# A scan-and-gate kernel with a written-out issue order: whole-row loads, an exclusive scan, two accumulator tiles and a new issue table

## The chip, the cores and the metric

The kernel runs on 1 core of one Trainium2 chip. The metric is the device time of one execution in microseconds (us). The core has TensorE (PE in the rows; its weight loads are PEld), VectorE (DVE), ScalarE (ACT), GpSimd (POOL) and SyncE (SP), which here issues all of the kernel's DMAs. All data are float32; matrices for large products are held as two float32r parts, high and low, and every large product is three matmuls (high x high, high x low, low x high).

## The reference

Two parts follow each other. The first is a linear recurrence for each batch `b` and head `h` (4 batches, 8 heads, 768 steps, 48 channels):

```python
for t in range(S):
    cur = np.einsum('bhd,bhe->bhde', u[None] * kt, vt)       # the bonus u
    y[:, :, t] = np.einsum('bhd,bhde->bhe', rt, state + cur)
    state = wt[:, :, :, None] * state + np.einsum('bhd,bhe->bhde', kt, vt)
```

The second takes y as `x` (4 x 768 x 384), computes `relu(x @ w_in)` with 1024 columns, halves it into u and v, normalizes v over its 512 columns, multiplies it by `w_spatial` (768 x 768) along the steps, adds `b_spatial`, gates u with it and multiplies by `w_out` (512 x 384).

## The kernel before, in words

The steps are cut into 24 slots (4 batches x 6 chunks of 128 steps). In a slot, `slot_load` (L372) brings W (the decays), kr (k and r) and v, from slot 6 on also N (k and r the other way round). `slot_prep` (L401) makes the recurrence a matmul: it multiplies neighbouring decays into W2 (L432), scales k and r (L435), runs two product scans of DVE, F from the end of each half chunk (L438) and E from its start (L444), and scales k by F (L450) and r by E (L454). As E holds products up to and including its step, r is multiplied by E one place further on, and the first place of each half chunk is multiplied by `z0` in an operation of its own (L447). `slot_a` (L507) multiplies k with r, `slot_kt` (L528) transposes k into KT, `slot_y` (L544) and `slot_inter` (L581) accumulate y, `slot_d`, `slot_s` and `slot_w` (L597 to L640) carry the state, `slot_x` (L644) adds y's two parts and transposes y into xT.

y is accumulated in one PSUM tile `pyw` (L277) of two banks: `slot_x` copies bank 0 to SBUF (L658) and then adds bank 1 (L660). Columns 384 and up of bank 0 are `pw`, into which `warm` (L878) multiplies zeros where TensorE has nothing to do.

The second part is units of work: `hv_unit` (L689: v and its statistics), `scale` (normalization), `g_unit` (L756: u, the product with `w_spatial`, the gate) and `out_unit` (L795: the last product, the copy L807 and the store L809). `split64` (L330) splits a weight matrix that arrives as float64 into its two parts: a load (L335), a first conversion (L350) and further operations; `prep_sp` (L320) does it for `w_spatial`.

**The order of the work is written out by hand.** Each operation names the engines on which it may run and a cost for each. The string `PLAN` (L31) has one word per operation, in the order in which the code names them: a letter for the engine (T, V, A, G, S for TensorE, VectorE, ScalarE, GpSimd, SyncE) and a due time in base 36, in hundredths of a us. `plan` (L198) sorts the operations by due time, and `issue` puts them out in that order, so each engine runs its own operations strictly in the table's order. An operation that waits holds up everything behind it on its engine. A due time is not waited for. `fill` (L882) puts a number of `warm` matmuls into gaps of TensorE's due times, up to a certain operation. A load can't be issued before the users of the buffer that it fills are done; v and W have two buffers each, kr has three.

Of the kernel before, what the change touches and what calls it, by code (L numbers as in the profile page):

```python
# [16 lines left out]
C = 128  # L17
# [14 lines left out]
Txx S4g Tfy Aij Vk8 S2i9 S1r9 S5k Alg Vo5 Vpe Vuo Awp G11w Sod A1ez V1k7 V1nq V1r4 A1t5 G1vn Sm5 A14o V1ba  # L32
V1dd V1l4 A1nc V1z7 S28 S3c S8w Vfx Tkv Vb4 Gis Vhl Vcd Gej Vfb Vij Vp2 Vmh Vku Ay5 A13b V2s V10g Tpt V13h Tol
Aq2 T128 T15q Tw8 Vzp A10t V16e T1ba A1cp V1ft T1k0 A1rw T1tg A1uu Sso A1qa V1uh V22j V2da A2if V2lm Szx A23g
V2cd V2px V2sk A2v8 V2ye Sq9 A1kh V1mt V1pf V1st A20n V2na S1se A3wa G3xy S3le A4lu V4y2 S22o A4ha V4j2 S4cf
A53w V55g S4fx A5d3 V5er S4nh A5by V5ks S576 A5ka V5oq S2ww A5nx V5rp S1p1 A2te V303 S5gj A5p2 V5t0 S4zt A5fd
G5x6 S5mi A5xe G6d7 S2ll A37y V3km V3n2 V3pc A44p V4re S2h5 V31e V3ab V3fk V3iy A3v5 V4lp S3r2 V4gn V4kd V4sq
V4ud A50e V5d5 S2uo A3d2 V4vo V4wr V5bu A5e8 V5hr T1we T1zf T21t A26f A2dx A2ek S7s S6o Sa0 Vr3 Tt8 Vtq Gwl
Vsr Vwc Gyi Vzd V11s V175 Gz1 G16m Ayu A16a G3m Vy1 T19t V1h4 A17h T143 A19z T1hl T1lk T1c4 V1f2 A1gk V1vf
T1na A1p9 V1w5 T1yb A1zl T21c A22e T26w T2gs T2j9 A2rh A2wn A2xb Sl1 Sn9 S1dw V19l T1oo V15g V1c7 G1fa V17f  # L40
V1d5 V1ix V1xh V1jm G1h8 V20v A251 A25q V276 T23q V28i A1wi T1ko A1m5 T2bt T2do T25i V2ab A2bf V2gy T2fe A2hd
V2it T2l6 A2mf T2oo A2pq T2rn T2tj T2vg A2zf A31p A32c A34t V35z V35r G3dw G3eo V3fd G3hm G3ie A3m4 A3tq G429
A3q0 A3zb G48k A3j3 A4cb G56z Syt S1cs S1nx G25e T29e V248 G29d V2be V25h G28u V2b2 V2f9 V2ez G2f7 G2vf A2uj
A2go V2k5 T30j V365 A2ju T2lx A2nh T2mt T3ao T2yt V331 A35c V389 T3ce A3fe V3gv T3jm A3l2 T3n7 A3o9 T3qz T3sw
T3vo A45u A484 A48s S1xv S1q5 S2g1 G2i2 T2p6 V2rm V2u9 V2oz V2wi V325 V32o V342 V33s G32l G36e A3t1 A2qs V2v7
T3f5 V3uc A39c T39s A3bu T3p4 T3xl T3ds V3i7 V3qn V3z5 T3zb A41a V42r T46v V48c T4ao A4dq T4fa T4h7 T4jl A4mz
A4p9 A4pw S2jd S2kh S3d1 V3b1 T3gm V39d V3re V3cq V3do G3h3 V3kb V3ld V3zw V3so G3uk A3pb A3ym V3w5 T40p V44t
V419 T3ut A3xf T450 T47k T426 V442 V47k T49a A4b9 V4cp T4el A4g8 T4j4 A4ks T4me T4oa T4q7 A4sp A4v0 A4vn A4y4
V505 V4ze V4zx V50n V516 V51p V528 A57i A5aj V5g3 V5ak A5gi V5j3 V52s A551 V5m3 T8xw S3ka A42c S456 A4if S4l9
A51j S54d A5hx T2xd T320 T340 A3gg T58v T5lw T5nc T5q8 T5ro T5t4 V5wx V62k A648 V6hy T35g T36w T38c A3ec T5br  # L50
T5d7 T5en T5kg T5os T5w0 V63w V68k A6dj V6k7 T3kb T3lr T3no A3rz T5yw T60c T61s T638 T664 T6dd V6fe G6lr A6oo
# [12 lines left out]
S5p5 S6vu S7q5 S837 G6og G779 V7bw V6vz V740 V75w V78w V7je V7cu G7jn V847 V85v V87i A9az V8z3 A8fm V89j V8fl
V93e A8g3 T8rw V94o V8zo T8d3 V8fq T9ev T8tc V90r G91z V96u T9gl A9sx V9w6 T9za Va0j Va26 Taet Tahz Tajw Aame
Aaoo Aapc S6km S862 S898 S8rz V7ay V8hc G8qo V7eu G7hg V7jp V7mq V94c G8is V8vf G8ln V8ol V8q8 V9zu A9is V8rv
A8rw A98i A8zj V9es T9hz V9tn G982 T9e0 A9hl Ta1r T9jg V9om G9rd V9sw Ta35 Aa6g Va7w Tahb Aaik Vak2 Tamh Taoe
Taqb Aast Aax3 Aay2 S7eb S8u7 S8t3 S9h9 G7vh G9fy V9as V8lv G8q5 V96h V9js V9c2 V9i5 V9mz V99h G9by V9fq G9so
A9s8 V9vo A9n4 A9he Ga0n G9ov T9zy Va5x Ga7y T9mu V9pd Tabq Ta4j Vab2 Vac4 Tadf Vafe Vah2 Talt Van6 Vaot Tas8
Tavl Taxi Ab06 Ab2h Ab3y Ab6f Vb7k Vb7d Vb7w Vb8f Vb8z Vb9h Vba1 Abdl Abfy Gbhw Vbbu Abif Gbpu Vbak Abc6 Gbe4  # L70
S9id A9v1 S9xv Aadc Sag6 Aauq Saxk Ab86 T9ku T9nq T9qm A9tz Tble Tbpq Tbsm Tbu2 Tc1b Tc5n Vc7w Vcj9 Acky Gcry
T9s2 T9ti T9uy Aa20 Tbfm Tbh2 Tbii Tbwz Tbyf Tc2r Vc4s Vcgg Acn4 Gcpa T9we T9xu Ta5d Aafp Tbjy Tbmu Tboa Tbr6
Tbvj Tbzv Vc1w Gc4v Ac7s Vcur Ta7d Ta8t Taa9 Aacb Tc73 Tc8j Tc9z Tccb Tcdr Tcf7 Vcr7 Vcxk Aczd Gd11 Td5o Td7o
Td94 Tdc1 Adfn Sdh5 Tdgd Tdht Tdll Tdn1 Vdp3 Se1q Tdal Tddh Tdex Tdj9 Adyt Se3x Tau5 Tazf Tb1r Ab6y Tc47 Tco1
Tcph Tcqx Tcse Tctu Vcz6 Vd62 Adnd Gdvs Tb6e Tbba Tbcq Abhd Te6i Teau Teca Tef7 Tegn Teir Vep9 Ger3 Aeu0 Vf8b
# [144 lines left out]
def kernel(  # L220
# [812 lines left out]
```

## Time and profile before

| what | value |
|---|---|
| median of 3 runs | 388.3 us (387.86 to 388.34) |
| the profiled execution | 388.89 us, of which the span from the first to the last instruction is 387.1 us |
| TensorE's mean granted clock | 0.977 of full speed |
| TensorE (PE), busy | 361.8 us, 93% |
| DMA, bytes | 47.76 MB, mean 123 GB/s |

A busy time is the time in which at least one instruction of the engine was under way. A row of the timeline reads: start in us from the span's start, duration, engine, line, operation, output and inputs, count of merged instructions, and in brackets the engine's idle time ahead of it with what ended it. "x82" counts every matmul instruction; a float32 matmul is two of them.

### The profile page before, as it was taken

Reading aid. Unit: us, or ns where it says so; the run is one execution under the profiler, and the core shown is the slowest. Engines: PE = TensorE matmul, PEld = TensorE weight load, DVE = VectorE, ACT = ScalarE, POOL = GpSimd, SP = SyncE. Lnnn points to the kernel's source line nnn. Section 1 sums busy time; section 2 is a strip of 40 time slices with the busy share of each in tenths; the row PEclk is TensorE's granted clock in tenths of the full one; section 3 lists DMA queues with packets and bytes.
Section 4 is the critical chain, followed back from the end, with each engine's and each line's share of the span. In section 5 each row is a group of like instructions: output and inputs, shape, how many; then the busy total and the mean of one; then the engine's idle time right before and its main releaser. Section 6 shows DMA issues by size and latency. Waiting matters only on the chain.

```text
span 387.1 us, 11326 instructions
## 1 busy us (share of the span) xinstructions
PE 361.8 (93%) x4648; PEld 331.3 (86%) x4648; DVE 294.2 (76%) x649; ACT 202.9 (52%) x563; POOL 126.8 (33%) x162
## 2 busy tenths in 40 slices
PE   7969959999988999999999899998999999999995
PEld 6857748889878989889888878888999998899995
DVE  7976867799998789767979899889887767414333
ACT  2555946987441746783353476772354355641311
POOL 3524321411234244546362233125242233041110
PEclk9997986999999999999999999999999999999999
DMA  7995474565144355641353536633245401100201
GB/s 203 266 248 155 119 222 128 155 186 158 37 140 125 110 172 159 204 126 61 87 157 87 176 99 164 195 109 88 51 135 169 142 22 45 41 22 0 68 35 66
DMA packets 29514, 47.76 MB, mean 123 GB/s; under 512 B 2450, under 2 KB 21010, under 8 KB 29458
## 3 DMA queue, kind: packets, MB, share of 16 engines
q1 hardware_dynamic: 29458, 47.00, 42.9%
q8 instruction: 37, 0.61, 0.7%
q14 instruction: 19, 0.16, 0.1%
HBM read 42.27 MB, written 4.72 MB: 121 GB/s over the span
## 4 chain that ended last, share of the span: by engine, by line
PE 49%; DVE 19%; DMA 15%; ACT 8%; issue 5%; POOL 1%; SPq 0%; ACTq 0%; DVEq 0%; POOLq 0%
PE pv L681 6%; DMA kr<-in_tr_dram 6%; PE pv L682 6%; PE pv L683 6%; DMA Nw<-in_gt_dram 5%; PE pyw L555 4%; DMA d_('wo', 0)_680<-in_w_out_dram 3%; PE ph L681 2%; PE ph L683 2%; PE ph L682 2%; PE pu L681 2%; PE pu L682 2%; PE pu L683 2%; PE po L681 2%; PE yt L664 2%
## 5 line engine op out<-in xcount | busy, mean ns | idle before, releaser
L681 PE MATMUL pv<-ws,vh 128*128 128x384 f32 x192 | 66.7, 347 | 6.5 <-ACT ot L807 2.2
L683 PE MATMUL pv<-ws,vl 128*128 128x384 f32 x192 | 64.8, 338 | 0.0
L682 PE MATMUL pv<-ws,vh 128*128 128x384 f32 x192 | 64.8, 338 | 0.0
L681 PEld LDWEIGHTS pv<-ws,vh 128*128 128x128 f32 x192 | 36.0, 188 | 9.4 <-ACT ot L807 2.5
L682 PEld LDWEIGHTS pv<-ws,vh 128*128 128x128 f32 x192 | 36.1, 188 | 0.0
L683 PEld LDWEIGHTS pv<-ws,vl 128*128 128x128 f32 x192 | 36.1, 188 | 0.0
L791 ACT CAST gh<-t 128x384 fp32r<-128x384 f32 x32 | 16.0, 512 | 36.7 <-DVE t L789 24.4
L787 DVE TENSOR_TENSOR t<-pv,b_sb 128x384 f32<-128x384 f32 x32 | 17.6, 551 | 22.9 <-PE pv L683 21.8
L681 PE MATMUL pu<-xT,wi 128*128 128x384 f32 x96 | 34.7, 362 | 0.0
L681 PE MATMUL po<-wo,gh 128*128 128x384 f32 x96 | 33.4, 348 | 0.1
L435 POOL TENSOR_TENSOR kr<-kr,W 112x256 f32<-112x256 f32 x23 | 22.8, 995 | 32.2 <-issue 10.8
L682 PE MATMUL pu<-xT,wi 128*128 128x384 f32 x96 | 32.8, 342 | 0.0
L683 PE MATMUL pu<-xT,wi 128*128 128x384 f32 x96 | 32.8, 341 | 0.0
L683 PE MATMUL po<-wo,gl 128*128 128x384 f32 x96 | 32.4, 337 | 0.0
L682 PE MATMUL po<-wo,gh 128*128 128x384 f32 x96 | 32.2, 336 | 0.0
L681 PE MATMUL ph<-wi,xT 128*128 128x512 f32 x72 | 30.8, 428 | 0.0
L683 PE MATMUL ph<-wi,xT 128*128 128x512 f32 x72 | 28.7, 398 | 0.0
L682 PE MATMUL ph<-wi,xT 128*128 128x512 f32 x72 | 28.6, 397 | 0.0
L636 ACT ACTIVATE S<-S,prod 112x48 f32<-112x48 f32 x84 | 21.2, 326 | 7.0 <-DVE S L626 6.7
L789 POOL TENSOR_TENSOR t<-t,us 128x384 f32<-128x384 f32 x10 | 10.6, 1065 | 39.0 <-DVE t L787 30.8
L710 ACT ACTIVATE hv<-ph 128x512 f32<-128x512 f32 x24 | 14.3, 595 | 15.4 <-PE ph L683 15.3
L611 PE MATMUL paw<-v,KT 64*64 64x48 f32 (+1 forms) x704 | 16.1, 216 | 5.1 <-ACT KT L542 5.1
(202 smaller groups left out, 968.2 us busy)
## 6 DMA issues: line engine op xcount, KB each, us to landing
kr<-in_tr_dram SPq DMA_DIRECT2D x24, 448.0 KB, 5.0
N<-in_nat_dram SPq DMA_DIRECT2D x18, 384.0 KB, 3.9
Nw<-in_gt_dram SPq DMA_DIRECT2D x16, 384.0 KB, 3.3
W<-in_tr_dram SPq DMA_DIRECT2D x24, 224.0 KB, 4.5
v<-in_nat_dram SPq DMA_DIRECT2D x24, 192.0 KB, 3.5
out_dram<-ot SPq DMA_DIRECT2D x24, 192.0 KB, 2.0
wst<-in_w_spT_dram SPq DMA_DIRECT2D x12, 192.0 KB, 5.1
d_('wv', 0)_146<-in_w_in_dram SPq DMA_DIRECT2D x1, 512.0 KB
```

The costliest lines, as they stand in the source:

```text
L435: op({"G": pool(half), "V": dve(half)}, lambda e, n=n: e.tensor_tensor(two(kr()[:, n])[:, :, n], two(kr()[:, n])[:, :, n], two(W())[:, :, ...
L555: nc.tensor.matmul(py()[L * a:L * (a + 1), row, D * n:D * (n + 1)], x, z, start=(a, row) not in started, stop=not left[0], skip_group_chec ...
L611: nc.tensor.matmul(pa()[rows, a, G * L + g * D:G * L + (g + 1) * D], KT()[ps, g, rows], v()[ps, hs], start=True, stop=True)
L636: e.mul(S1[i % 2][a][:, g, :], S0[:, g, :], Wc[:, g:g + 1])
L664: nc.tensor.matmul(yT()[:, k_, :], y()[:, k_ * P:(k_ + 1) * P], ident, start=k_ == 0, stop=k_ == KX - 1, is_transpose=True, skip_group_che ...
L681: nc.tensor.matmul(ps, ah, bh, start=first, stop=False)
L682: nc.tensor.matmul(ps, ah, bl, start=False, stop=False)
L683: nc.tensor.matmul(ps, al, bh, start=False, stop=last)
L710: op({"A": 0.79}, lambda: nc.scalar.activation(hv(), ph(), AF.Relu, accum_out=col(0)), r=[(ph, 0)], w=[(hv, 0), (s, 0, j)])
L787: op({"V": dve(HT)}, lambda: nc.vector.tensor_tensor(t1(), pv()[:, :HT], b_sb[:, tsl], ALU.add), r=[(pv, 0), ("b", 0)], w=[(t1, 0)])
L789: op({"V": dve(HT), "G": pool(HT)}, lambda e: e.tensor_tensor(t1(), t1(), us(), ALU.mult), r=[(us, 0)], w=[(t1, 0)], port=True)
L791: op({"A": act(HT)}, lambda: nc.scalar.copy(gh(), t1()), r=[(t1, 0)], w=[(gh, 0)])
```

## The change

1. `u_sb`, the bonus vector, is loaded in all its 128 rows by the second of its loads too, where that load left out row 0.
2. W is loaded in whole rows of 516 values (`W()` from `tr[b, c, :, 1:WE]`), where it was four pieces of 128 values a row; its readers step over the value between two pieces.
3. E becomes an exclusive product: W2 is held in one tile with a leading 0, the scan reads it one place earlier and takes the maximum after the multiplication. r is multiplied by E in one operation over all places (112x512 in place of 112x496), and the operation L447 is gone, once per slot, 24 in all.
4. `pyw` becomes two tiles of one bank each, `PY[0]` and `PY[1]`; `pw` is a part of `PY[0]`.
5. The three constants and the warm-up output of ScalarE become columns of one tile; the first memsets are two of 512 columns in place of one of 1024.
6. Some costs that the operations name are changed, as L710 from 0.79 to 0.61 and L713 from 0.86 to 0.70.
7. The table is new: 1,930 words in place of 1,954. By its letters, VectorE has 578 operations in place of 637, ScalarE 404 in place of 388, GpSimd 169 in place of 150, TensorE 624 and SyncE 155 as before. `fill` makes 51 `warm` matmuls of the new table's gaps and 39 of the old one's (two further ones are operations of the table).

```diff
-    pyw = psX.tile([P, 2, 512], F32, name="pyw")
-    pw = pyw[:, 0, DM:]
-    nc.vector.memset(pyw, 0.0)
+    W2p = p1.tile([R, G * C // 2 + 1], F32, name="W2p")
+    nc.gpsimd.memset(W2p[:, :1], 0.0)
...
+    PY = [psX.tile([P, 512], F32, name=f"py{n}") for n in range(2)]
+    pw = PY[0][:, DM:]
+    for t in PY:
+        nc.vector.memset(t, 0.0)
...
-        load(W, [0], lambda: nc.sync.dma_start(
-            W().rearrange("p (g t) -> p g t", t=C),
-            tr[b, c, :, 1:WE].rearrange("p (g t) -> p g t", t=C + 1)[:, :, :C]), R * G * C * 4)
+        load(W, [0], lambda: nc.sync.dma_start(W(), tr[b, c, :, 1:WE]), R * G * C * 4)
...
         op({"V": 0.69}, lambda: nc.vector.tensor_tensor_scan(
-            E().rearrange("p s t -> p (s t)"), zE, W2(), 0.0, ALU.max, ALU.mult),
-           r=[(W2, 0), ("z0", 0)], w=[(E, 0)])
-        op({"V": 0.19}, lambda: nc.vector.tensor_tensor(
-            seg(kr()[:, 1])[:, :, 0], seg(kr()[:, 1])[:, :, 0], z0.unsqueeze(2).broadcast_to([R, SUB * G, 2]),
-            ALU.mult), r=[("z0", 0)], w=[(kr, "r0")])
+            flat(E()), W2()[:, :half], zE, 0.0, ALU.mult, ALU.max), r=[(W2, 0), ("z0", 0)], w=[(E, 0)])
...
-        op({"V": 0.68, "G": 1.07}, lambda e: e.tensor_tensor(
-            seg(kr()[:, 1])[:, :, 1:], seg(kr()[:, 1])[:, :, 1:],
-            E()[:, :, :L2 - 1].unsqueeze(3).broadcast_to([R, SUB * G, L2 - 1, 2]), ALU.mult),
+        op({"V": 0.69, "G": 1.1}, lambda e: e.tensor_tensor(
+            seg(kr()[:, 1]), seg(kr()[:, 1]), E().unsqueeze(3).broadcast_to([R, SUB * G, L2, 2]), ALU.mult),
            r=[(E, 0)], w=[(kr, "r")], port=True)
...
-        py.make = lambda: pyw[:, :, :DM]
+        py.make = lambda: PY
...
         op({"A": act(DM, True), "V": dve(DM)}, lambda e: (e.copy if e is nc.scalar else e.tensor_copy)(
-            y(), py()[:, 0]), r=[(py, 0)], w=[(y, 0)])
-        op({"V": 0.56}, lambda: nc.vector.tensor_tensor(y(), y(), py()[:, 1], ALU.add), r=[(py, 0)], w=[(y, 0)])
+            y(), py()[0][:, :DM]), r=[(py, 0)], w=[(y, 0)])
+        op({"V": 0.56}, lambda: nc.vector.tensor_tensor(y(), y(), py()[1][:, :DM], ALU.add), r=[(py, 0)], w=[(y, 0)])
```

Words of the two tables that the prediction speaks of (due times in us, decoded):

| operation | before | after |
|---|---|---|
| first matmuls on the bonus vector (L921), TensorE | `Tfy` 5.74 | `Tgq` 6.02 |
| start of y of slot 1 (L565), TensorE | `T1hl` 19.29 | `T1ov` 21.91 |
| first `w_out` load into d (`d_('wo', 0)`, L335), SyncE | `S2ll` 33.69 | `S1je` 19.94 |
| its first conversion (L350), ScalarE | `A37y` 41.74 | `A2yj` 38.35 |
| v of slot 4 (L388), SyncE | `S2g1` 31.69 | `S2j9` 32.85 |
| W of slot 5 (L381), SyncE | `S2jd` 32.89 | `S2g8` 31.76 |
| KT of slot 4 (L542), ScalarE | `A3bu` 43.14 | `A3in` 45.59 |
| state product of slot 4 (L611), TensorE | `T3ds` 43.84 | `T3ml` 47.01 |
| v of slot 5 (L388), SyncE | `S3d1` 43.57 | `S3mk` 47.00 |
| its first use (before: ScalarE, L475; after: VectorE, L486) | `A3pb` 47.99 | `V3wv` 50.71 |
| last of the 96 products of `out_unit` (L801), TensorE | `Tql1` 344.53 | `Tqt9` 347.49 |

## Rows read from the trace of the kernel before

**Rows 1.** The page's first part: busy us, share of the span, instructions.

```profile
PE 361.8 (93%) x4648; PEld 331.3 (86%) x4648; DVE 294.2 (76%) x649; ACT 202.9 (52%) x563; POOL 126.8 (33%) x162
```

**Rows 2.** The page's fourth part: the chain of waits, by engine.

```profile
PE 49%; DVE 19%; DMA 15%; ACT 8%; issue 5%; POOL 1%; SPq 0%; ACTq 0%; DVEq 0%; POOLq 0%
```

**Rows 3.** Busy time by stretch: stretch, length, each engine's busy us, clock, DMA.

```profile
27.90:34.70 6.80, 6.47 (x27) 5.68 (x27) 4.37 (x9) 3.21 (x9) 2.50 (x2) 0.50 0.93 253
55.20:65.40 10.20, 6.79 (x83) 6.67 (x84) 7.49 (x17) 5.34 (x14) 2.11 (x4) 0.50 0.31 102
70.00:382.00 312.00, 302.86 (x3777) 280.23 (x3769) 240.85 (x528) 162.13 (x457) 103.96 (x125) 1.00 0.38 109
```

**Rows 4.** Timeline, TensorE's last product.

```profile
382.11 0.34 PE L681 MATMUL po<-wo,gh 128*128 128x384 f32 x1
```

**Rows 5.** Timeline, TensorE's first work.

```profile
2.88 4.63 PE L880 MATMUL pyw<-zk 128*128 128x128 f32 x20 [2.88 <-DVE pyw L279]
7.44 0.72 PE L921 MATMUL pu__174<-ones,u_sb 1*48 1x1 f32 x16
```

**Rows 6.** Timeline, TensorE from 19 to 34 us.

```profile
21.84 1.60 PE L880 MATMUL pyw<-zk 128*128 128x128 f32 x12 [1.71 <-DVE y L660]
23.28 0.81 PE L565 MATMUL pyw<-bv,ident 128*128 128x384 f32 x2
...
27.33 0.43 PE L555 MATMUL pyw<-S,kr 48*64 48x48 f32 x12 [1.57 <-issue]
...
31.53 1.65 PE L880 MATMUL pyw<-zk 128*128 128x128 f32 x6 [0.33 <-DVE y L660]
```

**Rows 7.** Timeline, ScalarE and VectorE on y of slot 0.

```profile
19.83 0.48 ACT L658 COPY y<-pyw 128x384 f32<-128x384 f32 x1 [0.69 <-PE pyw L555]
...
21.25 0.54 DVE L660 TENSOR_TENSOR y<-y,pyw 128x384 f32<-128x384 f32 x1
```

**Rows 8.** Timeline, TensorE's longest wait.

```profile
58.62 0.98 PE L611 MATMUL paw<-v,KT 64*64 64x48 f32 x30 [5.08 <-ACT KT L542]
```

**Rows 9.** Timeline, ScalarE ahead of it.

```profile
56.70 0.55 ACT L350 ACTIVATE e_('wo', 0)_811<-d_('wo', 0)_680 128x384 f32<-128x384 f32 x1 [5.23 <-DMA d_('wo', 0)_680<-in_w_out_dram]
...
58.05 0.51 ACT L542 COPY KT<-pt 128x448 f32<-128x448 f32 x1
```

**Rows 10.** Timeline, the loads that SyncE issues from 40 us on.

```profile
40.88 0.33 SPq L388 DMA_DIRECT2D v<-in_nat_dram  x1
...
42.12 3.14 SPq L381 DMA_DIRECT2D W<-in_tr_dram  x1
...
46.35 0.44 SPq L335 DMA_DIRECT2D d_('wo', 0)_680<-in_w_out_dram  x1
```

**Rows 11.** The page's sixth part: loads, count, KB, median us from issue to landing.

```profile
kr<-in_tr_dram SPq DMA_DIRECT2D x24, 448.0 KB, 5.0
N<-in_nat_dram SPq DMA_DIRECT2D x18, 384.0 KB, 3.9
...
W<-in_tr_dram SPq DMA_DIRECT2D x24, 224.0 KB, 4.5
v<-in_nat_dram SPq DMA_DIRECT2D x24, 192.0 KB, 3.5
```

**Rows 12.** Groups by line, VectorE: busy us, mean ns; idle before.

```profile
L432 DVE TENSOR_TENSOR W<-W 112x256 f32<-112x256 f32 x18 | 12.0, 665 | 2.3 <-DMA W<-in_tr_dram 2.2
...
L447 DVE TENSOR_TENSOR kr<-kr,zz 112x16 f32<-112x16 f32 x24 | 3.8, 160 | 0.2
```

**Rows 13.** Timeline, GpSimd and VectorE beside each other.

```profile
11.73 1.08 POOL L435 TENSOR_TENSOR kr<-kr,W 112x256 f32<-112x256 f32 x1 [4.11 <-DVE rk L411]
12.02 1.06 DVE L432 TENSOR_TENSOR W<-W 112x256 f32<-112x256 f32 x1
...
16.69 0.46 DVE L432 TENSOR_TENSOR W<-W 112x256 f32<-112x256 f32 x1
```

More of the change, by code (lines that the diff above doesn't have):

```diff
@@ L37 @@
[L37 to L51, printed above, removed]
@@ new lines @@
+T13o T15x Tx1 V10n A15e V1ej T18f A19v V1h2 T1s5 A1vc T1xl A23h Suq A1we V21n V2bl V2g0 A2qc G2xa Sng A1mu
+V1r1 V1sa V1uw A2gd V2i8 S1h0 A2kw V2n4 V2pq V2sq A2us V345 S2v6 A3to G496 S238 A3gn V439 S25r A34s V38c S3xz
+A4i8 V4r1 S4c7 A5nh V5qb S4ux A5gg V5ms S2sw A5tl G5yv S5jh A5uq V61n S1i4 A2o6 V2rf S5v7 A67e V6i0 S4jx A5af
+V5hp S4y9 A5l7 V6jc S1je A2yj V31r V32u V363 A3d0 V5co S2i5 A3ju V3m4 V3q7 V4h2 A53l V5j1 S2qm A3m6 V4gb V4pq
+V504 A5k2 V5o3 S4it V4wy V4zd V51f V55w A5mc V5rn T27w T29t T2e2 A2hs A2jk A2mh S5k S7s Sgo Vur Tyf Vlw Vwp
@@ L121 @@
+Tqkl Tqrt Tqt9 Aqvb Sqwv Vn8u Tnlb Vp1v
 """
@@ L273 @@
     z0 = zz[:R, 1, :, 0]
+    W2p = p1.tile([R, G * C // 2 + 1], F32, name="W2p")
+    nc.gpsimd.memset(W2p[:, :1], 0.0)
     AS = [p1.tile([P, 2, G, L], F32, name=f"AS{n}") for n in range(AB)]
     paw = psA.tile([P, 2, 512], F32, name="paw")
-    pyw = psX.tile([P, 2, 512], F32, name="pyw")
-    pw = pyw[:, 0, DM:]
-    nc.vector.memset(pyw, 0.0)
+    PY = [psX.tile([P, 512], F32, name=f"py{n}") for n in range(2)]
+    pw = PY[0][:, DM:]
+    for t in PY:
+        nc.vector.memset(t, 0.0)
     ident = cp.tile([P, P], F32, name="ident")
     make_identity(nc, ident)
-    ones = cp.tile([P, 1], F32, name="ones")
-    nc.gpsimd.memset(ones, 1.0)
-    eps = cp.tile([P, 1], F32, name="eps")
-    nc.gpsimd.memset(eps, EPS)
-    neg = cp.tile([P, 1], F32, name="neg")
-    nc.gpsimd.memset(neg, -1.0)
-    nc.scalar.activation(cp.tile([P, 1], F32, name="warm"), eps, AF.Sqrt)
+    few = cp.tile([P, 4], F32, name="few")
+    ones, eps, neg = (few[:, n:n + 1] for n in range(3))
+    for t, x in ((ones, 1.0), (eps, EPS), (neg, -1.0)):
+        nc.gpsimd.memset(t, x)
+    nc.scalar.activation(few[:, 3:], eps, AF.Sqrt)
     mneg = pm.tile([P, 512], F32, tag="hv", name="mneg", bufs=4)
@@ L425, in two, with flat, w_ @@
         def two(t):
-            return t.rearrange("p (n q) -> p n q", q=2)
+            return t.rearrange("p (g n q) -> p g n q", g=G, q=2)
         def seg(t):
             return t.rearrange("p (s n q) -> p s n q", n=L2, q=2)
+        def flat(t):
+            return t.rearrange("p s t -> p (s t)")
+        def w_():
+            return W().rearrange("p (g t) -> p g t", t=C + 1)[:, :, :C].rearrange("p g (n q) -> p g n q", q=2)
         half = G * C // 2
-        op({"G": pool(half), "V": dve(half)}, lambda e: e.tensor_tensor(
-            W2(), two(W())[:, :, 0], two(W())[:, :, 1], ALU.mult), r=[(W, 0)], w=[(W2, 0)], port=True)
-        for n, key in ((0, ["k"]), (1, ["r", "r0"])):
-            op({"G": pool(half), "V": dve(half)}, lambda e, n=n: e.tensor_tensor(
-                two(kr()[:, n])[:, :, n], two(kr()[:, n])[:, :, n], two(W())[:, :, 1 - n], ALU.mult),
-               r=[(W, 0)], w=[(kr, x) for x in key], port=True)
+        op({"G": 0.62, "V": dve(half)}, lambda e: e.tensor_tensor(
+            W2()[:, 1:].rearrange("p (g n) -> p g n", g=G), w_()[:, :, :, 0], w_()[:, :, :, 1], ALU.mult),
+           r=[(W, 0)], w=[(W2, 0)], port=True)
+        for n, key in ((0, "k"), (1, "r")):
+            op({"G": 0.9, "V": dve(half)}, lambda e, n=n: e.tensor_tensor(
+                two(kr()[:, n])[:, :, :, n], two(kr()[:, n])[:, :, :, n], w_()[:, :, :, 1 - n], ALU.mult),
+               r=[(W, 0)], w=[(kr, key)], port=True)
         op({"V": 0.69}, lambda: nc.vector.tensor_tensor_scan(
-            F().rearrange("p s t -> p (s t)")[:, ::-1], zF[:, ::-1], W2()[:, ::-1], 0.0, ALU.max, ALU.mult),
-           r=[(W2, 0)], w=[(F, 0)])
-        op({"V": 0.16, "G": 0.23}, lambda e: e.tensor_scalar(Wc, F()[:, :, 0], FLOOR, None, ALU.max),
+            flat(F())[:, ::-1], zF[:, ::-1], W2()[:, :0:-1], 0.0, ALU.max, ALU.mult), r=[(W2, 0)], w=[(F, 0)])
+        op({"V": 0.17, "G": 0.24}, lambda e: e.tensor_scalar(Wc, F()[:, :, 0], FLOOR, None, ALU.max),
            r=[(F, 0)], w=[("Wc", i)], port=True)
@@ L491, in slot_prep @@
         for n, (j_, src, dst) in enumerate(((0, slice(0, C), slice(0, C)), (1, *halves), (1, *halves[::-1]))):
-            op({"A": 0.17, "V": 0.14}, lambda e, j_=j_, src=src, dst=dst: (e.copy if e is nc.scalar else e.tensor_copy)(
+            op({"A": 0.19, "V": 0.165}, lambda e, j_=j_, src=src, dst=dst: (e.copy if e is nc.scalar else e.tensor_copy)(
                 dgs()[dst, j_], dg()[src, :H].rearrange("p (g j) -> p j g", j=2)[:, j_]), r=[(dg, 0)], w=[(dgs, n)])
@@ L503, in diag @@
                                     dgs()[:, j].unsqueeze(2).broadcast_to([P, G, L]), ALU.mult)
-            op({"G": 0.74, "A": 1.06, "V": 0.42}, diag, r=[(dgs, n) for n in ((0,), (1, 2))[j]], w=[(As, j)], port=True)
+            op({"G": 0.62, "A": 1.07, "V": 0.43}, diag, r=[(dgs, n) for n in ((0,), (1, 2))[j]], w=[(As, j)], port=True)
     def slot_a(i):
@@ L554, in mm @@
             left[0] -= 1
-            nc.tensor.matmul(py()[L * a:L * (a + 1), row, D * n:D * (n + 1)], x, z, start=(a, row) not in started,
+            nc.tensor.matmul(py()[row][L * a:L * (a + 1), D * n:D * (n + 1)], x, z, start=(a, row) not in started,
                              stop=not left[0], skip_group_check=True)
@@ L564, in bonus @@
                 started.update(((0, 0), (1, 0)))
-                nc.tensor.matmul(py()[:, 0], ident, bv(), start=True, stop=False, skip_group_check=True)
+                nc.tensor.matmul(py()[0][:, :DM], ident, bv(), start=True, stop=False, skip_group_check=True)
             op({"T": 0.67}, bonus, r=[(bv, 0)], w=[(py, 0)])
         elif i == B_PE:
-            op({"V": 0.42}, lambda: nc.vector.memset(py()[:, 0], 0.0), w=[(py, 0)])
+            op({"V": 0.42}, lambda: nc.vector.memset(py()[0][:, :DM], 0.0), w=[(py, 0)])
         def intra():
@@ L592, in inter @@
                         mm(a, 2 * g + j, j, kr()[rs, 1, g * C + a * L:g * C + (a + 1) * L], S1[i % 2][a][rs, g, :])
-        op({"T": 0.5 if c else 0.3}, inter, r=[(kr, "r"), (kr, "r0")] + [("S1", i % 2, a) for a in subs],
+        op({"T": 0.5 if c else 0.3}, inter, r=[(kr, "r")] + [("S1", i % 2, a) for a in subs],
            w=[(py, 0)], mode="64x64")
@@ L895, in range_check @@
         pk = buf(psA, [P, C], "py", "pk", 1)
-        pk.make = lambda: pyw[:, 0, :C]
+        pk.make = lambda: PY[0][:, :C]
         def low():
@@ L903, in low @@
             nc.vector.tensor_tensor(okr[:, 0:1], okr[:, 0:1], okr[:, 1:2], ALU.min)
-        op({"V": 0.9}, low, r=[("over", i) for i in range(B * G)] + [("Wc", i) for i in range(NS)] + [("S1", n, a) for n in range(2) for a in range(SUB)],
+        op({"V": 1.12}, low, r=[("over", i) for i in range(B * G)] + [("Wc", i) for i in range(NS)] + [("S1", n, a) for n in range(2) for a in range(SUB)],
            w=[("okr",)] + [("Wc", i) for i in range(NS)])
```

175 lines of the change are left out of this document (92 added, 83 removed).

## The prediction

> **What bounds the kernel now.** I read the page's busy shares first: TensorE has work under way for 361.8 of 387.1 us [rows 1], so a gain can only come from time in which it idles, runs slowly or does filler. The chain of waits [rows 2] says that the rest hangs on VectorE (19%) and DMA (15%), so next I asked for busy time by stretch. Two things stand there [rows 3]. From 70 to 382 us TensorE runs at 1.00 of its clock and is busy 302.86 of 312.00 us: 9.1 us are idle in all that time. Ahead of that it was granted 0.50 of the clock (1.2 of 2.4 GHz) twice, for 6.8 us and for 10.2 us, and in these it worked 6.47 and 6.79 us, so about half of each, 3.2 and 3.4 us, is lost to the clock. TensorE had just idled both times: 1.71 and 1.57 us before the first fall [rows 6], and 5.08 us around the second [rows 8].
>
> As the order is fixed, I then held the starts of single rows against the table's due times. The difference, which I call the lag, shows where time is lost. TensorE's first product on the bonus vector is due at 5.74 and starts at 7.44: 1.7 us late, behind 20 filler matmuls that began at 2.88 when the memset of `pyw` was done [rows 5]. y of slot 1 is due at 19.29 and starts at 23.28: 4.0 [rows 6]. The state product of slot 4 is due at 43.84 and starts at 58.62: 14.8 [rows 8]. The last product is due at 344.53 and starts at 382.11: 37.6 [rows 4]. So some 15 us are lost by 59 us, about 3 more by the end of the second slow stretch, and the remaining 20 trickle away over 320 us. The kernel is bound by TensorE's work plus what its queue loses when an operation ahead of it is late.
>
> **The change part by part.**
>
> *The new table by itself.* TensorE has the same 624 operations. Its last product is due at 347.49 in place of 344.53: with every lag as before, it ends 3.0 us later. That is a difference of two orders, not a time of the chip, but I charge it in full: **+3.0**.
>
> *Two tiles for y.* In the row at 21.84 filler waits until VectorE has added bank 1 (L660), though filler writes only into bank 0's free columns: the one tile makes them wait. ScalarE's copy of bank 0 was done at 20.31 (19.83 + 0.48), L660 at 21.79 [rows 7]. With two tiles the 1.60 us of filler can run from 20.3 to 21.9, under L660, and y of slot 1, which first writes bank 0, needs only the copy: it can start at 21.9 in place of 23.28, 1.4 us earlier. The row at 31.53 is the same pattern with 0.33 us of wait. Bounds: 0 if the new table's longer gap there is what counts, 1.7 with both. I take **-1.5**.
>
> *The wait of 5.08 us.* TensorE waits for KT of slot 4, which ScalarE copies at 58.05. In front of it on ScalarE stands the first conversion of a piece of `w_out`, which waits 5.23 us for its load and starts at 56.70, due at 41.74 [rows 9]. That load was due at 33.69 and issued at 46.35 because SyncE stood behind v of slot 4 (due 31.69, issued 40.88, when its buffer came free) and behind W of slot 5, whose issue alone took 3.14 us [rows 10]. In the new table this load is due at 19.94, ahead of v of slot 4 altogether, and its conversion at 38.35: 18.4 us between them in place of 8.0, where the late one took 10.35 us from issue to use (56.70 - 46.35). So this wait goes, and with it what followed: the 3.4 us of slow clock. What is late next is ScalarE's queue itself, which lagged some 10 us there anyhow, as the others did. Together 8.5; bounds 0 (it comes back elsewhere) and 8.5. I take **-8.5**, since both causes, the order behind v and the slow issue, are removed.
>
> *The first slow stretch.* It follows two waits, 1.71 us for L660, which goes, and 1.57 us for which the trace names no releaser. Bounds 0 and 4.8 (3.2 of clock, 1.57 of wait). I take half, **-2.5**.
>
> *The trickle after 70 us.* Idle time is 9.1 us [rows 3]. A part of it hangs on loads whose first user is due sooner than such a load lands. By the medians (kr 5.0, N 3.9, W 4.5, v 3.5 us [rows 11]), of the loads due after 60 us the old table has ten of them (4 kr, 4 N, 1 W, 1 v), the new one three (2 kr, 1 v). Bounds 0 and 9.1; I take half, **-4.5**.
>
> *VectorE's relief.* L447 goes: 24 x 160 ns = 3.8 us busy [rows 12], less 24 times 16 columns more in the product with E, some 0.02 us each by the costs that the code names. By the letters 35 further operations leave VectorE; at the 0.55 us of y's addition [rows 7] that is about 19 us more off its 294.2 us. ScalarE gets 16, GpSimd 19. VectorE is idle a quarter of the span, so I cost this at nothing of its own: TensorE hides it, and its effect on TensorE stands in the trickle. If the cover is gone, at a share of 19% of the chain [rows 2], it is worth at most 23 x 0.19 = 4.4 us.
>
> *W in whole rows, and the other edits.* W brings 224 KB in 4.5 us, v 192 KB in 3.5, N 384 KB in 3.9 [rows 11]: the quarter rows are dear, and a W may land up to 1 us sooner. Every W has slack of several us in the table, so the landing itself is worth nothing; the issue of 3.14 us, if it recurs, stands in front of the loads of slot 5, and is counted above. Strided reads of W, the exclusive scan (the same two operands and columns) and the product over 512 columns: between -0.1 and +0.1 us each, on VectorE or GpSimd, 0 taken. The bonus vector's row 0, arriving twice, is 1.5 KB: 0. The first memset is half as long, so filler may start at about 2.4 in place of 2.88, but it is one filler longer: 0.
>
> *Sum.* 388.9 (the profiled execution, 1.8 over its span; the median 388.3 is 0.6 lower) + 3.0 - 1.5 - 8.5 - 2.5 - 4.5 = 374.9. The median's side of it is 374.3, and I leave 0.7 for one small wait that the new order makes: **375 us**.
>
> A rule of the Trainium skill speaks against moving operations from VectorE to GpSimd. The trace first: beside a product of GpSimd (11.73 to 12.81), VectorE's L432 of 256 columns took 1.06 us; with GpSimd idle it took 0.46 [rows 13], and its mean over 18 is 665 ns [rows 12]. "SBUF — State Buffer", section "SBUF: two separate sides", says that the two engines share one pair of ports as an exclusive lock, and that whichever of a VectorE operation with two SBUF inputs and a GpSimd operation comes second waits for the whole of the first. By that rule the trace agrees: the longer one ends just after GpSimd's. What it would do here is the third rival.
>
> **The rivals.**
>
> 1. *The trickle goes almost wholly.* All 9.1 us of idle time after 70 us and the whole first slow stretch go: 374.9 - 4.6 - 2.3 = **368**. For it: ten tight loads become three, and VectorE loses some 23 us. Against it: much of the idle time has other releasers than loads.
> 2. *The early wait moves.* v of slot 5 is due at 47.00 and its first user is now VectorE at 50.71: 3.7 us, where a v lands in 3.5 by the median and where the old table had 4.4. If it lands as late as the piece of `w_out` did (10.35 us), VectorE holds up the state of slot 4 by 6.6 us, TensorE idles some 5, and the clock falls as it did: the 8.5 us come back, **383**. Against it: there are fewer bytes in front of it.
> 3. *The lock on the ports.* 19 more operations on GpSimd each hold up VectorE by the 0.60 us between the two rows: 11.4 us. At VectorE's 19% of the chain that is 2.2 us, **377**; if all of it reached TensorE, **386**. Against it: VectorE has slack, and 59 operations fewer to be held up.
> 4. *Slower: DMA sets the pace of the first 66 us, whatever the order.* In the first slow stretch DMA was 0.93 busy [rows 3]. If TensorE waits there for bytes and not for places in a queue, the lags up to 66 us stay, the 3.0 us of the new table come on top, and the later queue, fuller on ScalarE, idles as before: 388.9 + 3.0 = **392**. It decides if the transfers ahead of slot 4's KT land later than about 55 us (KT's due time of 45.6 and a lag of 9). Against it: in the second slow stretch DMA was only 0.31 busy, and the late load was issued late, not carried slowly.
> 5. *It doesn't do what it says:* filler still waits for L660 with two tiles, as the wait might come from the order of the engine and not from the tile. Then the 1.5 and the 2.5 us stay: **379**.
>
> **How the numbers follow.** The forecast, with its own range of 370 to 380 (rival 5 and the lower end of rival 3 lie in it), has 0.52. Rival 1 has 0.13, rivals 2 and 3 in their dear form 0.17 together, rival 4 0.13, and 0.05 is left for sums that cancel. The range from **366 to 387** takes in all but rival 4, the cancelling sums and the edge of rival 1: about 0.8. A change of under 0.2% (0.8 us) can't be told from none here. Faster 0.82 (forecast, rivals 1 to 3), the same 0.04, slower 0.14 (rival 4 and a little of the cancelling).
>
> **What would show it.** Right: no row of TensorE around 45 to 55 us with a wait for KT of several us; no second stretch at 0.50 of the clock, and a shorter first one or none; filler in slots 0 to 2 that doesn't wait for the addition of bank 1; the lag of the last product at about 21 us (37.6 - 17.0) in place of 37.6; idle time after 70 us near 4.6; VectorE's busy time near 271 us. Wrong: a wait of 5 us on another load in the first 70 us, with the clock falling behind it; idle time after 70 us of 9 us or more; VectorE's products beside GpSimd longer on the mean than 665 ns for L432's; a lag of over 34.6 us, from which on the new table is the slower one.

## The result, and the profile after

The changed kernel takes **371.48 us** (median of 4 runs, 369.75 to 371.94) against 388.08 (384.25 to 388.34) for the kernel before in the same batch: ratio 0.9586, 95% interval 0.9519 to 0.9653. The forecast was 375.0 with a range of 366 to 387. An execution more than 1.5% above the fastest of its kernel is left out of all times and ratios here. The profiled execution took 371.31 us, with a span of 369.6.

The page's first part and its chain, for the kernel after (answering [rows 1, 2]):

```profile
PE 357.2 (97%) x4672; PEld 330.0 (89%) x4672; DVE 276.1 (75%) x591; ACT 211.9 (57%) x585; POOL 137.2 (37%) x182
PE 83%; DVE 7%; ACT 5%; issue 2%; POOL 1%; DVEq 0%; ACTq 0%; POOLq 0%
```

TensorE is now 83% of the chain in place of 49%, and DMA (15% before) is gone from it. Busy time by stretch, columns as in [rows 3]:

```profile
0.00:70.00 70.00, 64.43 (x1041) 54.22 (x1042) 60.58 (x127) 46.47 (x124) 27.63 (x44) 1.00 0.72 201
70.00:363.40 293.40, 292.74 (x3633) 275.73 (x3631) 215.53 (x465) 164.94 (x461) 109.59 (x139) 1.00 0.39 114
```

After 70 us TensorE idles for 0.66 us, where it idled for 9.14 [rows 3]; ahead of that the clock stays at 1.00. Its waits, longest first (waiting line, releasing line, us in total, times, longest):

```profile
PE py L880 <- DVE py L281: 2.3, 1, 2.3
PE py L880 <- ACT y L658: 1.1, 2, 0.6
PE ph L681 <- DVE bv L486: 0.7, 1, 0.7
```

The state product of slot 4 [rows 8] and the last product [rows 4], in the timeline after:

```profile
52.67 0.67 PE L611 MATMUL paw<-v,KT 64*64 64x48 f32 x32
...
362.77 0.34 PE L681 MATMUL po<-wo,gh 128*128 128x384 f32 x1
```

Due at 47.01 and 347.49, they come 5.7 and 15.3 us late, where the lags were 14.8 and 37.6. The loads [rows 11] and VectorE's product of two Ws [rows 12]:

```profile
kr<-in_tr_dram SPq DMA_DIRECT2D x24, 448.0 KB, 5.1
N<-in_nat_dram SPq DMA_DIRECT2D x18, 384.0 KB, 3.4
...
W<-in_tr_dram SPq DMA_DIRECT2D x24, 225.8 KB, 3.2
v<-in_nat_dram SPq DMA_DIRECT2D x24, 192.0 KB, 3.9
...
L437 DVE TENSOR_TENSOR W2p<-W 112x256 f32<-112x256 f32 x14 | 7.5, 537 | 0.4 <-DMA W<-in_tr_dram 0.2
```

**Where the time came from.** A lag is counted against a table, so lags of two tables can't be subtracted stretch by stretch. I therefore also worked out a *loss*: the time of a moment, less the costs (as the code names them) of all TensorE operations begun by then. 622 of its 624 operations (the other two are filler) cost 321.4 us in every kernel here. The loss falls by 6.3 us up to 72 us and by 13.6 behind (34.3 + 27.0 before, 28.0 + 13.4 after). What follows the start of TensorE's last operation grew from 4.3 to 6.8 us. Together that is -17.4; the spans differ by 17.5 (387.1 - 369.6). Some 0.6 us of the last two terms is a matter of counting: in the old table the last operation is the small product of the range check (L907), begun 0.62 us behind the last product, while the new table has it at 320 us. Counted to the last product, the terms are 13.1 and 1.9.

### The profile page after: what moved, and what is told of

The parts are those of the page before. It is cut to its first block, busy times and chain, and to the rows that moved or that the text cites. A ratio compares the mean times of both kernels' runs of the same rounds, so it can differ in the third digit from the quotient of the medians.

```text
span 369.6 us, 11375 instructions
## 1 busy us (share of the span) xinstructions
PE 357.2 (97%) x4672; PEld 330.0 (89%) x4672; DVE 276.1 (75%) x591; ACT 211.9 (57%) x585; POOL 137.2 (37%) x182
## 4 chain that ended last, share of the span: by engine, by line
PE 83%; DVE 7%; ACT 5%; issue 2%; POOL 1%; DVEq 0%; ACTq 0%; POOLq 0%
PE pv L681 9%; PE pv L682 9%; PE pv L683 9%; PE py L555 6%; PE po L681 5%; PE py L880 4%; PE po L683 4%; PE po L682 4%; PE ph L681 4%; PE pu L681 4%; PE ph L683 4%; PE ph L682 4%; PE pu L682 4%; PE pu L683 4%; PE paw L520 3%
## 5 line engine op out<-in xcount | busy, mean ns | idle before, releaser
L681 PE MATMUL pu<-xT,wi 128*128 128x384 f32 x96 | 34.4, 358 | 0.0
L683 PE MATMUL pu<-xT,wi 128*128 128x384 f32 x96 | 32.5, 339 | 0.1
L682 PE MATMUL pu<-xT,wi 128*128 128x384 f32 x96 | 32.4, 338 | 0.0
L500 ACT ACTIVATE AS<-id,dgs 128x64 f32<-128x64 f32 x76 | 20.1, 336 | 5.6 <-DVE dgs L492 5.5
L451 POOL TENSOR_TENSOR kr<-kr,F 112x496 f32<-112x496 f32 x13 | 15.4, 1187 | 17.6 <-DVE kr L441 9.1
L636 ACT ACTIVATE S<-S,prod 112x48 f32<-112x48 f32 x76 | 19.2, 323 | 4.6 <-DVE S L626 3.1
L455 POOL TENSOR_TENSOR kr<-kr,E 112x512 f32<-112x512 f32 x13 | 16.6, 1277 | 13.5 <-DVE kr L441 5.4
L789 POOL TENSOR_TENSOR t<-t,us 128x384 f32<-128x384 f32 x9 | 9.6, 1068 | 31.6 <-DVE t L787 30.0
```

Of the source, the lines that this page charges most:

```text
L451: op({"V": 0.68, "G": 1.07}, lambda e: e.tensor_tensor(seg(kr()[:, 0])[:, :, :L2 - 1], seg(kr()[:, 0])[:, :, :L2 - 1], F()[:, :, 1:].unsqu ...
L455: op({"V": 0.69, "G": 1.1}, lambda e: e.tensor_tensor(seg(kr()[:, 1]), seg(kr()[:, 1]), E().unsqueeze(3).broadcast_to([R, SUB * G, L2, 2]) ...
L500: e.mul(As()[:, j, g, :], id64, dgs()[:, j, g:g + 1])
L636: e.mul(S1[i % 2][a][:, g, :], S0[:, g, :], Wc[:, g:g + 1])
L681: nc.tensor.matmul(ps, ah, bh, start=first, stop=False)
L682: nc.tensor.matmul(ps, ah, bl, start=False, stop=False)
```

## The experiments

Ratios are to the kernel before on the same chip, with 95% intervals; 388 us times the difference gives the us. Here is the loss of TensorE in each profiled execution, up to 72 us and from there to its last operation:

```
kernel                                   up to 72   behind
before                                     34.3      27.0
before, bonus vector in 128 rows           26.4      28.8
before, new table                          30.0      16.7
after, old table                           24.9      26.3
after, old times, new engines              25.4      27.9
after, new times, old engines              30.0      25.8
after, bonus vector in 127 rows            28.0      17.1
after, second reciprocal                   28.7      14.3
after                                      28.0      13.4
```

**Code or table.** The kernel after with the due times and engines of the table before, and the kernel before with those of the table after. The load of `w_out` shows the edit to the tables:

```diff
-S1je
+S2ll
```

> The changed code with the old table (its 24 words for the removed operation L447 taken out). Theory A, the table: most of the gain is the order, so this keeps the wait of some 5 us for KT of slot 4 and the second slow stretch, and gains only what two tiles give early: 382 to 386 us. Rival B, the code: two tiles, whole-row W (SyncE no longer stands 3 us on one issue) and 24 operations fewer carry it: 371 to 376 us.

> The old code with the new table (a word for L447 put in behind each scan E). Theory A: 373 to 378 us, no second slow stretch, idle time after 70 us near 2 us as in the changed kernel. Rival B: 383 us or more, with filler waiting for L660 and W landing late.

Code alone: 377.96 us (376.83 to 379.18), ratio 0.9778 [0.9702, 0.9854]. Table alone: 375.76 (373.54 to 377.13), 0.9708 [0.9632, 0.9784]. The first lies between the ranges of its two theories, so neither held; the second is as its theory A had it. Either removes the wait of 5 us, so the order of the loads, on which I put it, is not the only thing that makes it. With the code alone SyncE issues W of slot 5 at 37.99 in 0.37 us, from the *old* places. The trickle behind 72 us goes with the table: 26.3 with the old one, 16.7 with the new.

**One tile for y, and W in four pieces, in the kernel after.**

```diff
-    PY = [psX.tile([P, 512], F32, name=f"py{n}") for n in range(2)]
+    pyw = psX.tile([P, 2, 512], F32, name="pyw")
+    PY = [pyw[:, n] for n in range(2)]
...
-        load(W, [0], lambda: nc.sync.dma_start(W(), tr[b, c, :, 1:WE]), R * G * C * 4)
+        load(W, [0], lambda: nc.sync.dma_start(
+            W().rearrange("p (g t) -> p g t", t=C + 1)[:, :, :C],
+            tr[b, c, :, 1:WE].rearrange("p (g t) -> p g t", t=C + 1)[:, :, :C]), R * G * C * 4)
```

> The changed kernel with y's two banks in one tile again. Theory A: filler and the start of y of slots 1 and 2 wait for L660: 1.5 to 3 us more than the changed kernel (373 to 374.5), and a slow stretch early if the wait is over 1.5 us (then 376). Rival: the new table's longer gaps there take it up: under 0.7 us.

> The changed kernel with W loaded in four pieces a row again, into the same places. Theory A: W's slack in the table hides it: within 0.8 us of the changed kernel, W landing in some 4.5 us in place of 3.2. Rival B: the many pieces fill the queue, SyncE stands on W again for some 3 us, and the loads behind come late: 374 us or more, with a new wait in the first 70 us.

One tile: 370.86 us (369.91 to 372.98), 0.9592 [0.9522, 0.9662]. W in pieces: 371.09 (369.79 to 374.23), 0.9595 [0.9524, 0.9667]. Neither is told from after. In the first, TensorE's waits on bank 1's addition come back:

```profile
PE pyw L880 <- DVE y L660: 1.2, 1, 1.2
PE pyw L565 <- DVE y L660: 0.8, 1, 0.8
```

So the tiles separate as predicted. They take these 2.0 us of waits away, put 0.7 us of waits on the copy of bank 0 (L658) in their place, and save no time. In the second run W, in its four pieces, lands in 3.5 us by the median and not in the 4.5 that I expected; in after it is 3.2.

**Parts alone in the kernel before: one load moved, W in whole rows, two tiles.** The first moves one word, the first load of `w_out`, from 33.69 to 27.00; the others put the lines of the change in.

```diff
-S2ll
+S230
```

> The kernel before with one word of its table changed: the first load of w_out is due at 27.00 in place of 33.69, ahead of v of slot 4. Theory A (this load's place behind v makes the wait of 5.08 us and the slow stretch behind it): 377 to 379.5 us, no slow stretch at 55 us, lag at 64 us of about 9 in place of 17.6. Rival (the queue is late anyway: the next late operation on ScalarE or the next load takes its place): 383 us or more, with another wait of TensorE before 66 us.

> The kernel before with W in whole rows and nothing else but the constants in one tile, for space. The code with the old table lost the wait of 5 us too, so one of its parts must do it. Theory A (the 3.1 us in which SyncE stood on W's many pieces): the wait goes, 378 to 380.5 us, W's issue near 0.4 us. Rival (the tiles): the wait stays, 384 us or more.

> The kernel before with y's banks as two tiles and nothing else. Theory A: 1.5 to 4 us less than before by the early filler, but SyncE still stands on W and the wait of 5 us stays: 382 to 384.5 us. Rival (the early lag of 4 us is what makes v of slot 4 late, and with it everything behind): the wait goes, 378 us or less.

Load early: 382.9 us (380.68 to 383.88), 0.9843 [0.9745, 0.9940]. W in rows: 387.57 (385.19 to 390.85), 1.0004 [0.9961, 1.0047]. Two tiles: 387.59 (386.71 to 389.16), 0.9988 [0.9956, 1.0020]. The second has the time of its rival (the wait stays); the first lies between its two theories, and the third gained nothing where I expected 1.5 to 4 us. Moving the load takes the wait away, but SyncE still stands 3.37 us on W, and the clock is at its lower level from 54.4 to 61.2 us. Whole rows do not shorten that issue, so W's pieces are not its cause. SyncE in the kernel with whole rows:

```profile
40.24 0.29 SPq L928 DMA_DIRECT2D u_sb<-in_u_rep_dram  x1
40.63 3.34 SPq L379 DMA_DIRECT2D W<-in_tr_dram  x1
44.07 0.39 SPq L380 DMA_DIRECT2D kr<-in_tr_dram  x1
```

What stands in front of W in all three, and in before, is the load of rows 1 to 127 of the bonus vector. That gave a new theory.

**The engines or the times of the new table.** With the kernel after, the second copy of v of slot 5 (L475) shows the two crossings (new word `V41h`, old `A3ym`): old times on the new engines, then new times on the old engines.

```diff
-V41h
+V3ym
...
-V41h
+A41h
```

> The changed code with the old table's due times and the new table's engines (282 operations stand on another engine, 35 fewer on VectorE). With the old table whole it was 378.0 us and lost 19 us of lag after 72 us. Theory A (the order and its room are what ends the trickle): 376 to 380 us, 15 us or more of late lag. Rival (fewer operations on VectorE end it): 372 us or less, late lag under 10 us.

> The kernel after with the new due times, but every operation that has a counterpart goes to the engine that it had in the table before (282 operations differ). Theory A (the order of TensorE's work against its operands ends the trickle after 70 us, not the placement on engines): 371 to 375 us, lag at the end 15 to 19. Rival B (both are needed, the times were chosen for these engines): 376 to 381 us, lag at the end 20 to 27, with new short waits on VectorE or GpSimd.

Old times, new engines: 381.31 us (380.85 to 384.25), 0.9831 [0.9735, 0.9927]. New times, old engines: 384.58 (382.36 to 386.91), 0.9910 [0.9868, 0.9953]. Both are dearer than the whole new table on this code (0.9586); against the whole old one (0.9778) the first can't be told from it, and the second is dearer, with intervals that don't meet. The first lies above the range of its theory A, the second above the ranges of both its theories. Theory A of the second was wrong: the order needs its engines. Without them VectorE works 293.5 us in place of 276.1, and TensorE waits again behind 72 us (longest of its waits in 72 to 380 us):

```profile
PE pt L538 <- DVE kr L451: 1.9, 1, 1.9
PE ph L681 <- DVE t L787: 1.3, 2, 0.9
PE yt L664 <- ACT ph L713: 1.0, 1, 1.0
```

**The bonus vector's rows.** One line, in the kernel before, and undone in the kernel after (there the lines change places):

```diff
-    op({"S": 0.45}, lambda: nc.sync.dma_start(u_sb[1:], u_rep[1:]), r=[("u1", 0)], w=[("u", 0)], dma=0.55)
+    op({"S": 0.45}, lambda: nc.sync.dma_start(u_sb, u_rep), w=[("u", 0), ("u1", 0)], dma=0.55)
```

> The kernel before with one edit: the bonus vector is loaded into all 128 rows instead of rows 1 to 127; table, W's pieces, banks and scan stay. Theory A (the load of 127 rows goes through one DMA engine, and SyncE stands behind it; that is the wait of 5.08 us and the slow clock after it): SyncE issues W in well under 1 us, the wait for slot 3's transposed keys goes below 1 us, the slow stretch of 10.2 us goes, the lag at 72 us falls from 18.2 to about 9 to 11, and the time is 377 to 381 us, 7 to 11 below before. Rival B (the wait comes from the order of loads in the old table): nothing moves, 386 to 390 us, SyncE still stands 3 us on W. Rival C (the wait goes but the trickle after 70 us is what is left of it): below 375 us.

> The kernel after with the bonus vector loaded into rows 1 to 127 again, where the new table has it (due 63.77). Theory A (one DMA engine and a blocked SyncE wherever it is issued): SyncE stands 3 us or more on the issues behind it, but the loads due behind it at that place have more slack than in the table before; 372 to 375 us, 1 to 4 above after. Rival B (only the place in the table matters): SyncE's issues stay short and the time is within 0.8 us of after. Rival C: the wait comes back whole with a slow stretch of the clock, 378 to 382 us.

128 rows in the kernel before: 379.86 us (three runs, 378.84 to 382.83), 0.9783 [0.9678, 0.9887]. 127 rows in the kernel after: 374.36 (372.61 to 375.45), 0.9639 [0.9557, 0.9721], 2.9 us over after by the medians, 2.1 by the ratios. That interval overlaps after's, so the 2 to 3 us are likely and not certain; the kernel with a second reciprocal, in the same batch, took 371.80. Theory A holds in both, but for the length of SyncE's stand in the second. SyncE in the kernel before with 128 rows, where each of these issues is short:

```profile
37.03 0.43 SPq L929 DMA_DIRECT2D u_sb<-in_u_rep_dram  x1
37.56 0.38 SPq L381 DMA_DIRECT2D W<-in_tr_dram  x1
38.04 0.43 SPq L384 DMA_DIRECT2D kr<-in_tr_dram  x1
38.52 0.42 SPq L335 DMA_DIRECT2D d_('wo', 0)_680<-in_w_out_dram  x1
```

In before, W's issue takes 3.14 us there [rows 10]. The wait of 5.08 us and the 10.2 us at the lower clock level are gone from the profile with 128 rows; two stretches of 3.4 us at that level (from 61.8 and 109.6 us on) stand in it. The loads of the 10 us from that issue of the bonus vector on: what the DMA engines moved in 40 slices of 0.25 us (busy tenths of all 16 engines, then GB/s), and then each load's KB and its us to landing. First before (41.7 to 51.7 us):

```profile
DMA  4589996952000000267998936989999958999978
GB/s 61 111 283 406 332 283 270 393 197 43 0 12 25 31 25 25 39 115 145 293 283 172 231 106 188 326 319 401 365 283 281 225 135 240 350 348 301 332 256 266
...
W<-in_tr_dram SPq DMA_DIRECT2D x2, 224.0 KB, 11.1
kr<-in_tr_dram SPq DMA_DIRECT2D x1, 448.0 KB, 10.3
d_('wo', 0)_680<-in_w_out_dram SPq DMA_DIRECT2D x1, 384.0 KB, 10.3
```

Then before with 128 rows (37 to 47 us):

```profile
DMA  3699769999999997599798999979999999999793
GB/s 55 184 313 344 197 221 356 369 313 332 320 293 322 311 213 213 215 360 270 234 303 262 279 291 295 275 197 332 344 375 377 318 287 250 221 197 207 141 227 98
...
W<-in_tr_dram SPq DMA_DIRECT2D x2, 224.0 KB, 5.0
kr<-in_tr_dram SPq DMA_DIRECT2D x1, 448.0 KB, 6.5
d_('wo', 0)_680<-in_w_out_dram SPq DMA_DIRECT2D x1, 384.0 KB, 6.8
...
u_sb<-in_u_rep_dram SPq DMA_DIRECT2D x1, 192.0 KB, 4.4
```

The reader is to see the hole in the first: for seven slices (1.75 us, from 44.2 us on) 0 to 39 GB/s move, 25 in three of them, and SyncE stands until 45.26. From 44.58 to 45.90 us the trace has only packets of 1,536 bytes, the length of a row of the bonus vector: 22 of them, each begun 0.061 us after the one before and 0.065 us long, so one at a time. At that rate the 190.5 KB of 127 rows take 7.8 us, which is an estimate; the 128 rows land in 4.4. And the loads issued in the 8 us behind the 127 rows take 10 to 12 us to land, where they take 5 to 7 behind 128. Where the edit acts, from 36 to 72 us, the loss grows by 10.6, 11.4 and 12.9 us in the three kernels with 127 rows and the load of `w_out` in its old place (before, W in rows, two tiles), and by 7.0, 4.9 and 5.0 in the three with 128 rows and the old due times. In the profiled execution with 128 rows another 4.3 us are gone by 36 us, before the edit can act, so that part is not its work. The kernel after with 127 rows, where the load comes at 72.72, shows the same rate (72.5 to 82.5 us) and SyncE standing on the next issue:

```profile
GB/s 172 319 381 412 375 334 246 197 258 234 55 25 25 166 129 307 197 25 25 25 31 258 160 86 270 332 406 426 422 340 231 225 127 143 117 18 68 166 289 291
...
73.10 2.05 SPq L324 DMA_DIRECT2D wst<-in_w_spT_dram  x1
```

Its loss grows by 5.1 us from 72 to 100 us, where after's grows by 1.2, with 3.4 us at 0.51 of the clock from 88.2 on. I forecast a stand of 3 us or more; it was 2.05. Over all profiles, the issue next behind 127 rows takes 2.05 to 3.90 us in all six kernels that load them so, and 0.36 to 0.38 in all eight that load 128. An issue of over 1 us alone proves nothing, as there are such without that load too, up to 2.50 us (a store, code alone). Not run was a load of another number of rows from row 1 on, so its start at row 1 is not told apart from its count of 127.

The Trainium skill, "DMA: Bandwidth & Descriptors", section "Why a DMA increments its semaphore by 16 and not by 1", states that a load uses as many DMA engines as the largest number up to 16 that divides the slowest dimension of both its sides: 128 partitions use 16, 127 use one. The trace agrees, by the packets that come one at a time and by the rate: 25 GB/s under no other load, against a sum of 300 and more. That SyncE's later issues stall behind such a load is in the rows above, not in that section.

**VectorE's slack.** The kernel after with one more reciprocal a slot (the `is` only puts both into one operation):

```diff
-            flat(E()), W2()[:, :half], zE, 0.0, ALU.mult, ALU.max), r=[(W2, 0), ("z0", 0)], w=[(E, 0)])
+            flat(E()), W2()[:, :half], zE, 0.0, ALU.mult, ALU.max) is nc.vector.reciprocal(z0, Wc), r=[(W2, 0), ("z0", 0)], w=[(E, 0)])
```

> The kernel after with one more reciprocal per slot on VectorE (the kind that the change removes, about 0.2 us each, some 4.9 us in 24 slots) behind the second scan. Theory A (VectorE has slack: its work of 276 us in 370 is not what TensorE waits for): within 1 us of after, 370.5 to 372.5 us. Rival B (VectorE is close to the bound behind the order, and the removed operations are part of the gain): 374 to 377 us, with TensorE's waits on VectorE back.

371.80 us (370.31 to 373.11), 0.9575 [0.9494, 0.9657], with VectorE at

```profile
PE 357.6 (96%) x4672; PEld 330.0 (89%) x4672; DVE 280.5 (76%) x615; ACT 211.7 (57%) x585; POOL 137.4 (37%) x182
```

4.4 us more work on VectorE cost nothing that can be measured: theory A. So the removed operation of 3.8 us [rows 12] is no measurable part of the gain.

## Why the prediction came out right, step by step

The direction and the size hold (375.0 against 371.48), and most of what was to show it came: no wait for KT, no second slow stretch, no filler behind the addition of bank 1; the lag at the end is 15.3 and not 20.6, the idle time after 70 us 0.66 and not 4.6. But the causes were partly others, and the sum is as near as it is because errors cancel, which is luck: early, 9.5 us were forecast (the new table's 3.0 counted there) and 6.3 came, behind 72 us 4.5 and 13.6, and 2.5 at the end stood in no term.

- **The bonus vector, 0: the term that was mis-sized.** I priced its row 0 as "1.5 KB: 0", by its bytes. The one line is worth 0.0217 x 388 = 8.4 us in the kernel before (4.4 to 12.5 by the interval; 3.6 to 8.0 by the loss from 36 to 72 us). In the kernel after, where it is undone, it is worth 2.1 to 2.9, if anything.
- **The wait of 5.08 us, -8.5: a size within the bounds, wrong cause.** I blamed the order of loads behind v and "the slow issue" of W. The slow issue and the landings of 10 to 12 us behind it came from the 127 rows. The order matters as a second way out: the one load moved early removes the wait too (0.0157 x 388 = 6.1 us, by the interval 2.3 to 9.9), and the new table issues the bonus vector at 72.92, behind the tight stretch. The two remedies overlap, so the parts don't add up: the code gives 2.2% alone and 1.2% (0.9708 - 0.9586, with intervals that just overlap) on top of the table.
- **The trickle, -4.5, measured -13.6: mis-sized.** I took 9.1 us of idle time as the bound and half of it as the term. Idle time is too small a measure: where the start of a matmul follows the one before by 0.25 us or more beyond the usual distance (the lower quartile for its line), what is beyond adds up to 12.1 us in before behind 70 us, and to 1.2 in after. The row of a matmul lasts longer than the distance to the next start (0.34 and 0.17 us in the last product), so it hides a part of each wait. Due times and engines of the table bring it together; either alone brings next to nothing (27.9 and 25.8 against 26.3). The chain speaks for a part of the loads, as I argued: behind 70 us that of before passes nine times through a load (kr, N and the loads that check the decays, 3.1 to 5.6 us each), that of after never. What each of them cost is not shown.
- **The table by itself, +3.0: holds** as far as can be seen: up to 72 us the code loses 28.0 with the new table and 24.9 with the old.
- **Two tiles, -1.5: the wait goes, no time comes.** Alone and undone it is within 0.8 us of nothing by the medians, and the interval of the run alone leaves at most 1.7 us of gain.
- **The first slow stretch, -2.5: not settled.** It is gone in after, but also in the run that only changes the bonus vector, whose edit acts 10 us later, and the run with W in pieces, on the new table, has 3.4 us at the lower level from 31.8 on; so it is not the same in every execution.
- **W in whole rows, 0: holds**, as neither run moved. But the quarter rows are hardly dear, against my reading of [rows 11]: on the new table W lands in 3.3 (old code) to 3.5 us in pieces and in 3.2 in rows, on the old one in 3.6 (two tiles) to 4.5 and in 3.9. Most of the fall from 4.5 to 3.2 goes with the table. **VectorE, 0 of its own: holds** for 4.4 us more; for the 17.4 us between the two placements it wasn't tried by itself, and with the old engines the new times lose 13 us. It came to 276.1 us and not near 271, since the 58 operations gone cost 0.31 us each and not 0.55.
- **The end:** 1.9 us more behind the last product, which I did not foresee. Between the last copy (L807) and the end of the span lie 3.7 us in all profiles with the old due times and 5.4 to 6.0 in all seven with the new ones. SyncE stands there at the closing branch (L975): by the view of its waits 0.5 us in before and 3.3 in after, where the longest wait is 2.8. What ends that wait the trace does not say, so the cause stays open.
- **A reading:** the 20 filler rows at 2.88 us [rows 5] are 10 matmuls, as each is two instructions; no term hangs on it.

Of the rivals, the first (368, the trickle almost gone) came true in its mechanism; what it had wrong are the early gain (11.8 us forecast, 6.3 measured), the trickle's size (9.1 and 13.6) and the end. The early wait did not move to v of slot 5. The lock on the ports is not seen as a loss: with 20 more operations on GpSimd the mean of VectorE's product of Ws fell from 665 to 537 ns and that of its product with E rose from 666 to 840 (the longest 1,562), while 4.4 us more on VectorE cost nothing. DMA did not set the pace: with nearly the same bytes the loss fell.

## What to carry to other kernels

When an issue takes 3 us and the loads behind it land at twice their median, look at the load issued ahead of it and at the number of its rows, not at the late one's size. Price a transfer by how it is spread over DMA engines as well as by its bytes. In an order written out by hand, due times and placement are one choice: test them together, and measure waits by gaps between starts rather than by idle time.

## What the runs showed of the hardware beyond what was expected

- A load of 127 rows of 1,536 bytes moved at about 25 GB/s where nothing else moved, one packet at a time, and SyncE stood 2.05 to 3.90 us on the next issue, in six kernels of both codes; with 128 rows the same load lands in 3.7 to 4.4 us in eight kernels, and the next issue takes 0.36 to 0.38 us.
- TensorE's clock fell to its lower level in the wait of 5.08 us, for 10.2 us; in after it stayed at 1.00 from start to 363 us without a wait longer than 0.7 us between the first filler and the end, except the filler's own.
- W in rows of 2,064 bytes lands in 3.2 us and in pieces of 512 bytes in 3.5, for the same values on the new table; this kernel has no use for the difference.
